# The first three pairs of weight loads move to ScalarE's DMA queue, and the weight conversions start one attention unit sooner

## The chip, the core and the metric

The kernel runs on one core of a Trainium2 chip. Its time is the device time of one execution in microseconds; the kernel before has a median of 679.96 us over three runs (679.66 to 681.74). A profile is one further execution, recorded instruction by instruction; its durations are compared with its own span, not with the median.

The engines are called as in the profile: PE is TensorE (matmuls; PEld are its weight loads), DVE is VectorE, ACT is ScalarE, POOL is GpSimd and SP is SyncE, which here does nothing but start DMA transfers. SPq and ACTq are the queues of SP and ACT seen as starters of transfers.

## The reference

What is computed is a decaying linear attention, whose result goes straight into a feed-forward layer with a softplus:

```python
state = zeros((B, H, D, D))                       # B, H, S, D = 4, 8, 768, 64
for t in range(S):
    state = gamma[:, None, None] * state + outer(k[:, :, t], v[:, :, t])
    y[:, :, t] = D ** -0.5 * (q[:, :, t] @ state)
x = y.transpose(0, 2, 1, 3).reshape(B * S, H * D) # 3072 tokens x 512
h = x @ w_in                                      # 512 x 2048
out = softplus(h) @ w_out                         # 2048 x 512
```

q, k and v are float32. The weights w_in and w_out are float64, and each load brings their 64-bit words as they are.

## The kernel before

**Attention units.** The sequence of a batch is cut into six chunks of 128 tokens, and each chunk into two halves of four heads: 48 units, worked one after the other. The first twelve units load q, k and v by tokens (`load_unit`, L148 to L164; the DMA itself is L153, 128 KB each for kn, qn and vn). On the way to its output a unit needs, in this order: POOL multiplies q and v by decay factors (L172, L177); PE transposes k and q (`operands`, L186, tile tp); ACT and DVE copy them out of PSUM (kz L188 and L189, qs L190); PE forms the scores (`scores`, L217, tile sc); ACT copies them (L218, tile a); POOL masks them (L225); PE multiplies by v (`outputs`, L280 and L283, tile yp); ACT and DVE split the result into two float32r parts, xh (L284) and xl (L285). `new_state` (L245, tile stp) and `stack_state` (L261, stw) carry the state from chunk to chunk.

**The feed-forward part.** The 2048 hidden columns are cut into 16 slices f of 128. For a block of 256 or 384 tokens, `hidden` (L330 to L332, tile hp) multiplies xh and xl by the slice of w_in, ACT and DVE form the softplus (L337 to L346, tiles sp, gh, gl), and `second` (L361 to L363, tile acc) multiplies by the slice of w_out. The first block of 256 tokens can start when the units of its first two chunks have their xh and xl, that is after units 0 to 3; the first hp matmuls need units 0 and 2 alone. The block takes slices 0 to 9 first, then the second block all sixteen.

**Weights.** `load_weights(f)` starts two transfers of 512 KB: 128 columns of w_in (L70, tile win) and 128 rows of w_out (L71, tile wout). `convert_weights(f)` makes from the 64-bit words two float32r tiles, winhl and wouthl, each a high and a low part: ACT scales the high words (L86, and L92 for wout), DVE shifts and joins (L94 to L96), ACT rounds to the high part (L98), and POOL subtracts to get the low part (L99). A slice costs five instructions on ACT's list, five on DVE's and two on POOL's. From slice FETCH = 3 on, a load is held until the ACT cast L98 of three slices earlier is done (the "pace" dependency).

**Order.** The program is written as ticks, four to a unit (`tick`, L314 to L318). Before the first feed-forward step a loop runs the ticks for the first units and starts weight loads and conversions between them; in it, slice 0 is loaded when the tick counter stands at -5, slices 1 and 2 at 3 and 7, and from 11 on each fourth tick converts a slice and loads another: slice 0 at 11, slice 1 at 15, slice 2 at 19. After that `convert_to` keeps the conversions ahead of the steps. A scheduler, which sorts by its own estimate of when things are ready, lays the written order out as one list for each engine, and each engine works strictly down its list.

**Waits of transfers.** Every transfer signals one of eight completion counters, DMAHW0 to DMAHW7, given out in turn. A transfer that takes a counter over waits at its place in the list until the transfer that had it before has landed. What stands behind it in the same list waits with it.

Of the kernel before, what the change touches and what calls it, by code (L numbers as in the profile page):

```python
# [17 lines left out]
P = 128  # L18
# [10 lines left out]
FETCH = 3  # L29
# [4 lines left out]
def decay_attention_then_softplus_ffn(ctx: ExitStack, tc: tile.TileContext, q, k, v, w_in, w_out, qtab, vtab, gtab, out):  # L34
    nc = tc.nc
# [3 lines left out]
    ND = DM // P  # L39
# [24 lines left out]
    raw, win, wout, converts = {}, {}, {}, {}  # L64

    def load_weights(f):
        fs = slice(f * P, (f + 1) * P)
        raw[f] = [const.tile([P, ND * P], I64, name=nm, tag=f"{nm}{f}") for nm in ("win", "wout")]
        loads_of_f = (
            nc.sync.dma_start(raw[f][0].rearrange("p (c w) -> p c w", c=ND), w_in[:, fs].rearrange("(c p) w -> p c w", p=P)),  # L70
            nc.sync.dma_start(raw[f][1], w_out[fs, :]),  # L71
        )

        if f >= FETCH:
            for load, after in zip(loads_of_f, converts[f - FETCH]):
                tc.add_manual_dep(load.ins, after.name, mybir.DependencyInfo(mybir.DependencyClass.Sync, mybir.DependencyReason.SCHED_ONLY), reason="pace")
# [237 lines left out]
    def tick(n):  # L314
        for at, part in PARTS.items():
            u, r = divmod(n - at, PERIOD)
            if r == 0 and 0 <= u < len(units):
                part(u)  # L318
# [69 lines left out]
    def ticks_for(i):  # L388

        return min(PERIOD * 2 * int(FIRST[i + 1] // C) + max(PARTS) - PERIOD + 1 + AHEAD, last_tick + 1)  # L390

    done, loaded, converted = FIRST_TICK, 0, 0

    def convert_to(n):
        nonlocal loaded, converted
        while converted < min(NF, n):
            convert_weights(converted)
            converted += 1
            if loaded < NF:
                load_weights(loaded)  # L400
                loaded += 1
# [6 lines left out]
    nc.scalar.dma_start(vtabs[:, 0], vtab)  # L408
    nc.scalar.dma_start(gtab_sb[lo, 0], gtab)
    nc.scalar.dma_start(gtab_sb[up, 0], gtab)  # L410
    make_identity(nc, ident)
    for par, own, oth in sides:
        nc.gpsimd.memset(kz[oth, par], 0.0)
# [24 lines left out]
    while done < ticks_for(0):  # L438
        tick(done)
        done += 1  # L440
        if done % 4 == 3 and done > 0 or done < 0 and loaded == 0:
            if loaded >= FETCH:
                convert_weights(converted)
                converted += 1
            load_weights(loaded)
            loaded += 1

# [69 lines left out]
```

## Time and profile before

| | us |
|---|---|
| median of three runs | 679.96 |
| the profiled execution | 688.11 |
| its span, first to last instruction | 686.0 |
| PE busy in the span | 661.4 |
| DVE / ACT / POOL busy | 433.2 / 357.2 / 315.0 |

The profiled execution is 8.15 us longer than the median, and 2.1 us of it lie outside the span. All times below are counted from the span's start. In a row of the timeline the columns are: start, duration, engine, line, operation, output and inputs, and in brackets the idle time of the engine just before it with what ended that. A duration of several merged instructions is that of the group. In a row of windows the columns are: the window, its length, the busy time of each engine with the number of instructions, the granted PE clock, the busy share of the 16 DMA engines and the rate in GB/s.

### The profile page before, as it was taken

The numbers are of one execution on the slowest core, as the hardware profiler recorded it, in microseconds if no ns is written. First come the engines' busy times: TensorE is split into PE (matmuls) and PEld (weight loads), VectorE is DVE, ScalarE is ACT, GpSimd is POOL, SyncE is SP. The second block draws the span as 40 slices with busy tenths as digits, with TensorE's granted clock in tenths as the row PEclk, the third lists the DMA queues.
The fourth block names the chain that finished last, engine by engine and source line by source line (L and its number), as shares of the span: only waits on it lengthen the run. The fifth ranks groups of instructions, "written<-read, shape, count | busy, mean of one in ns | idle before, by whom it ended". The sixth has DMA issues, their size and how long they took to land.

```text
span 686.0 us, 12848 instructions
## 1 busy us (share of the span) xinstructions
PE 661.4 (96%) x4136; PEld 601.1 (88%) x4136; DVE 433.2 (63%) x843; ACT 357.2 (52%) x808; POOL 315.0 (46%) x354
## 2 busy tenths in 40 slices
PE   6899999998999999999999899999999899999997
PEld 5788898988999899989999899999999799999996
DVE  5777788677556676775676766786656755432321
ACT  5787766545454555654555555564555545422221
POOL 5787667534343544454355344545343443332221
PEclk9999999999999999999999999999999999999999
DMA  8897561222221241222122122222222111000100
GB/s 241 221 292 215 164 177 36 50 68 67 46 38 36 37 102 30 40 40 71 37 39 55 35 78 42 36 50 41 73 38 39 34 31 47 1 1 0 47 1 32
DMA packets 153827, 46.76 MB, mean 68 GB/s; under 512 B 140448, under 2 KB 148640, under 8 KB 153760
## 3 DMA queue, kind: packets, MB, share of 16 engines
q1 hardware_dynamic: 153312, 45.93, 28.1%
q8 instruction: 33, 0.54, 0.3%
q14 instruction: 34, 0.28, 0.1%
q10 hardware_dynamic: 448, 0.01, 0.0%
HBM read 39.60 MB, written 6.29 MB: 67 GB/s over the span
## 4 chain that ended last, share of the span: by engine, by line
PE 70%; SPq 8%; DMA 8%; DVE 5%; issue 4%; ACT 3%; POOL 2%; POOLq 0%; DVEq 0%; ACTq 0%
PE hp L330 10%; PE hp L332 10%; PE hp L331 10%; PE acc L361 10%; PE acc L363 10%; PE acc L362 10%; SPq L136 7%; DMA win<-in_moe_w_in_dram 2%; DMA vn<-in_v_dram 2%; PE sc L223 2%; PE stp L245 2%; DMA qb<-in_q_dram 1%; DVE kq L200 1%; PE yp L296 1%; PE yp L297 1%
## 5 line engine op out<-in xcount | busy, mean ns | idle before, releaser
L346 POOL TENSOR_TENSOR gl<-sp,gh 128x384 fp32r<-128x384 f32 (+1 forms) x120 | 130.8, 1090 | 227.8 <-ACT gh L344 198.9
L330 PE MATMUL hp<-xh,winhl 128*128 128x384 f32 (+1 forms) x576 | 186.0, 323 | 2.1 <-DVE sp L342 0.9
L332 PE MATMUL hp<-xh,winhl 128*128 128x384 f32 (+1 forms) x576 | 185.3, 322 | 0.9 <-POOL winhl L99 0.9
L331 PE MATMUL hp<-xl,winhl 128*128 128x384 f32 (+1 forms) x576 | 184.7, 321 | 0.0
L361 PE MATMUL acc<-wouthl,gh 128*128 128x512 f32 x384 | 153.1, 400 | 0.2 <-ACT gh L344 0.2
L362 PE MATMUL acc<-wouthl,gh 128*128 128x512 f32 x384 | 151.8, 396 | 0.0
L363 PE MATMUL acc<-wouthl,gl 128*128 128x512 f32 x384 | 150.7, 396 | 0.1
L338 ACT ACTIVATE sp<-sp 128x384 f32<-128x384 f32 (+1 forms) x120 | 65.3, 545 | 138.0 <-DVE sp L337 137.8
L330 PEld LDWEIGHTS hp<-xh,winhl 128*128 128x128 f32 x576 | 109.4, 190 | 6.5 <-ACT winhl L98 1.0
L331 PEld LDWEIGHTS hp<-xl,winhl 128*128 128x128 f32 x576 | 109.5, 190 | 3.8
L332 PEld LDWEIGHTS hp<-xh,winhl 128*128 128x128 f32 x576 | 109.4, 190 | 1.6 <-POOL winhl L99 1.3
L337 DVE TENSOR_SCALAR sp<-hp 128x384 uint32<-128x384 uint32 (+1 forms) x120 | 68.6, 574 | 63.2 <-PE hp L332 62.0
L344 ACT CAST gh<-sp 128x384 fp32r<-128x384 f32 (+1 forms) x120 | 64.0, 534 | 74.0 <-DVE sp L342 50.1
L342 DVE SCALAR_TENSOR_TENSOR sp<-hp,sp 128x384 f32<-128x384 f32 (+1 forms) x120 | 69.5, 579 | 35.8 <-ACT sp L338 34.9
L363 PEld LDWEIGHTS acc<-wouthl,gl 128*128 128x128 f32 x384 | 71.9, 188 | 14.8 <-POOL gl L346 0.5
L361 PEld LDWEIGHTS acc<-wouthl,gh 128*128 128x128 f32 x384 | 72.4, 189 | 11.1 <-ACT gh L344 0.3
L362 PEld LDWEIGHTS acc<-wouthl,gh 128*128 128x128 f32 x384 | 72.5, 189 | 10.8
L225 POOL TENSOR_SCALAR_AFFINE_SELECT a<-a 128x512 f32<-128x512 f32 x48 | 35.1, 730 | 43.2 <-DVE a L224 39.3
L224 DVE TENSOR_REDUCE a<-sc 128x256 f32<-128x512 f32 x72 | 48.8, 679 | 7.1 <-PE sc L223 4.1
L230 POOL TENSOR_TENSOR al<-a,ah 128x512 fp32r<-128x512 f32 x36 | 47.8, 1327 | 9.3 <-ACT ah L229 9.1
L200 DVE TENSOR_TENSOR kq<-kb,kq 64x256 fp32r<-64x256 f32 x72 | 45.3, 629 | 3.2 <-ACT kq L199 1.0
L195 DVE STREAM_TRANSPOSE kb<-kb 128x256 f32<-128x256 f32 x36 | 16.0, 445 | 49.3 <-DMA kb<-in_k_dram 37.9
(81 smaller groups left out, 993.1 us busy)
## 6 DMA issues: line engine op xcount, KB each, us to landing
win<-in_moe_w_in_dram SPq DMA_DIRECT2D x16, 512.0 KB, 5.0
wout<-in_moe_w_out_dram SPq DMA_DIRECT2D x16, 512.0 KB, 4.5
vn<-in_v_dram SPq DMA_DIRECT2D x48, 128.0 KB, 2.8
out_dram<-o SPq DMA_DIRECT2D x24, 256.0 KB, 2.2
kb<-in_k_dram SPq DMA_DIRECT2D x288, 16.0 KB, 1.7
qb<-in_q_dram SPq DMA_DIRECT2D x288, 16.0 KB, 1.7
vn<-in_k_dram SPq DMA_DIRECT2D x30, 128.0 KB, 2.3
kn<-in_k_dram SPq DMA_DIRECT2D x12, 128.0 KB, 3.9
```

What stands on the lines that cost most here:

```text
L200: nc.vector.tensor_tensor(kq[oth, 0, par], kt[own], kq[own, 0, par].bitcast(F32), op=ALU.subtract)
L330: nc.tensor.matmul(hp[:, k], lhsT=wt[:, 0, d, :], rhs=xh[:, d, :], start=d == 0, stop=False)
L331: nc.tensor.matmul(hp[:, k], lhsT=wt[:, 0, d, :], rhs=xl[:, d, :], start=False, stop=False)
L332: nc.tensor.matmul(hp[:, k], lhsT=wt[:, 1, d, :], rhs=xh[:, d, :], start=False, stop=d == ND - 1)
L337: nc.vector.tensor_scalar(sp.bitcast(U32), hps[s].bitcast(U32), 0x80000000, None, op0=ALU.bitwise_or)
L338: nc.scalar.activation(sp, sp, AF.Softplus)
L342: nc.vector.scalar_tensor_tensor(g, hps.pop(s), 0.0, g, op0=ALU.max, op1=ALU.add)
L344: nc.scalar.copy(gh, g)
L346: nc.gpsimd.tensor_tensor(gl, sps.pop(s), gh.bitcast(F32), op=ALU.subtract)
L361: nc.tensor.matmul(acc[i][t], lhsT=gh[:, k, ts], rhs=wt[:, 0], start=begins and k == 0, stop=False)
L362: nc.tensor.matmul(acc[i][t], lhsT=gh[:, k, ts], rhs=wt[:, 1], start=False, stop=False)
L363: nc.tensor.matmul(acc[i][t], lhsT=gl[:, k, ts], rhs=wt[:, 0], start=False, stop=ends and f == fs[-1])
```

## The change

The transfers of slices 0, 1 and 2 are started by ACT, right behind the four small table loads with which ACT's list begins, instead of by SP between the loads of the first units. The loop of ticks then converts and loads from counter 7 on, so slices 0 to 3 are converted at 7, 11, 15 and 19 (before: slices 0 to 2 at 11, 15 and 19).

```diff
@@ load_weights(f)
+        queue = nc.scalar if f < FETCH else nc.sync
         loads_of_f = (
-            nc.sync.dma_start(raw[f][0]..., w_in[:, fs]...),
-            nc.sync.dma_start(raw[f][1], w_out[fs, :]),
+            queue.dma_start(raw[f][0]..., w_in[:, fs]...),
+            queue.dma_start(raw[f][1], w_out[fs, :]),
         )
@@ after the four table loads on nc.scalar
+    for _ in range(FETCH):
+        load_weights(loaded)
+        loaded += 1
@@ while done < ticks_for(0):
         tick(done)
         done += 1
-        if done % 4 == 3 and done > 0 or done < 0 and loaded == 0:
-            if loaded >= FETCH:
-                convert_weights(converted)
-                converted += 1
+        if done % 4 == 3 and done > 4 * FETCH - 8:
+            convert_weights(converted)
+            converted += 1
             load_weights(loaded)
             loaded += 1
```

In the changed kernel all lines behind the first edit have numbers that are higher by 1 to 4. The lists below give, for each place, the row of the list, the line, the operation with its tiles (a number behind a name tells copies of a tile apart), and in brackets the counters and engines waited for.

**ACT at the start of the program.** Before, the first copy of unit 0 stands behind the table loads:

```order
L409 DMA gtab_sb_77<-in_gtab_dram 64x8
L410 DMA gtab_sb_77<-in_gtab_dram 64x8
L188 COPY kz_86<-tp_140 64x256 [waits PE_49]
L190 COPY qs_87<-tp_140 128x256 [waits DVE_49]
L261 COPY stw0_88<-stp_93 64x2x64 [waits DVE_49]
L218 COPY a_155<-sc_156 128x512 [waits PE_49]
L86 ACTIVATE win_134<-win_134 128x512 [waits DMAHW2_49]
```

And now:

```order
L411 DMA gtab_sb_77<-in_gtab_dram 64x8
L71 DMA win_108<-in_moe_w_in_dram 128x4x128 [waits DMAHW1_49]
L72 DMA wout_109<-in_moe_w_out_dram 128x512 [waits DMAHW3_49]
L71 DMA win_112<-in_moe_w_in_dram 128x4x128 [waits DMAHW5_49]
L72 DMA wout_113<-in_moe_w_out_dram 128x512 [waits DMAHW7_49]
L71 DMA win_116<-in_moe_w_in_dram 128x4x128 [waits DMAHW1_49]
L72 DMA wout_117<-in_moe_w_out_dram 128x512 [waits DMAHW3_49]
L189 COPY kz_86<-tp_148 64x256 [waits PE_49]
L262 COPY stw0_88<-stp_93 64x2x64 [waits DVE_49]
L87 ACTIVATE win_108<-win_108 128x512
L87 ACTIVATE wout_109<-wout_109 128x512
L191 COPY qs_87<-tp_148 128x256 [waits DVE_49]
```

Six transfers now stand ahead of the first copy. Counters 1, 3, 5 and 7 are those of ACT's four table loads; the third win takes over counter 1 from the first win, and the third wout counter 3 from the first wout. The activations of win_108 and wout_109 have no wait of their own any more, because ACT has waited for both landings by then.

**SP behind the loads of units 0 and 1.** Before, the rows from the last load of unit 1 on are:

```order
L153 DMA vn1_91<-in_v_dram 128x4x64 [waits DMAHW1_49]
L70 DMA win_134<-in_moe_w_in_dram 128x4x128 [waits DMAHW2_49]
L71 DMA wout_135<-in_moe_w_out_dram 128x512 [waits DMAHW3_49]
L153 DMA kn_148<-in_k_dram 128x4x64 [waits DMAHW4_49,PE_49]
L153 DMA qn_150<-in_q_dram 128x4x64 [waits DMAHW5_49,Pool_49]
L153 DMA vn2_92<-in_v_dram 128x4x64 [waits DMAHW6_49]
L70 DMA win_163<-in_moe_w_in_dram 128x4x128 [waits DMAHW7_49]
```

Now the loads of unit 2 follow those of unit 1 directly, then seven small loads of a table (qblocks), and then come these rows, the last two of the seven first:

```order
L434 DMA qblocks_80<-in_qtab_dram 32x4x1 [waits DMAHW0_49]
L434 DMA qblocks_80<-in_qtab_dram 32x4x1 [waits DMAHW1_49]
L71 DMA win_223<-in_moe_w_in_dram 128x4x128 [waits DMAHW2_49,Activation_49]
L434 DMA qblocks_80<-in_qtab_dram 32x4x1 [waits DMAHW3_49]
L154 DMA kn_190<-in_k_dram 128x4x64 [waits DMAHW4_49,PE_49]
L154 DMA qn_192<-in_q_dram 128x4x64 [waits DMAHW5_49,PE_49,Pool_49]
```

win_223 is slice 3, and kn_190 and qn_192 belong to unit 3. The row of qblocks ahead of kn_190 takes counter 3, which the third wout on ACT had before it.

**ACT around the first softplus.** Slice 4's cast is `winhl_517` in both. Before, it stands behind the first two softplus activations and the first gh:

```order
L338 ACTIVATE sp_404<-sp_404 128x512 [waits DVE_49]
L86 ACTIVATE win_373<-win_373 128x512 [waits DMAHW4_49]
L188 COPY kz_86<-tp_467 64x256 [waits PE_49]
L344 CAST gh_408<-sp_404 128x512 [waits DVE_49]
L338 ACTIVATE sp_459<-sp_459 128x512 [waits DVE_49]
L284 CAST xh_82<-yp_475 128x2x128 [waits PE_49]
L86 ACTIVATE wout_374<-wout_374 128x512 [waits DMAHW1_49]
L98 CAST winhl_517<-w_513 128x512 [waits DVE_49]
```

And now:

```order
L87 ACTIVATE win_337<-win_337 128x512 [waits DMAHW6_49]
L262 COPY stw1_89<-stp_93 64x2x64 [waits DVE_49]
L285 CAST xh_82<-yp_351 128x2x128 [waits PE_49]
L219 COPY a_369<-sc_370 128x512 [waits PE_49,Pool_49]
L99 CAST wouthl_392<-w_388 128x512 [waits DVE_49,Activation_49]
L87 ACTIVATE wout_338<-wout_338 128x512 [waits DMAHW1_49]
L99 CAST winhl_517<-w_513 128x512 [waits DVE_49]
L93 ACTIVATE wp_521<-wout_280 128x512
L339 ACTIVATE sp_426<-sp_426 128x512 [waits DVE_49]
```

Slice 4's cast has moved ahead of the first softplus, and xh of unit 3 (made from `yp_351`) has slice 5's first activation (`win_337`) ahead of it. On PE the two lists differ up to about row 490 of 3942, matmul by matmul; behind that they are the same.

More of the change, by code (lines that the diff above doesn't have):

```diff
@@ L68, in load_weights @@
         raw[f] = [const.tile([P, ND * P], I64, name=nm, tag=f"{nm}{f}") for nm in ("win", "wout")]
+        queue = nc.scalar if f < FETCH else nc.sync
         loads_of_f = (
-            nc.sync.dma_start(raw[f][0].rearrange("p (c w) -> p c w", c=ND), w_in[:, fs].rearrange("(c p) w -> p c w", p=P)),
-            nc.sync.dma_start(raw[f][1], w_out[fs, :]),
+            queue.dma_start(raw[f][0].rearrange("p (c w) -> p c w", c=ND), w_in[:, fs].rearrange("(c p) w -> p c w", p=P)),
+            queue.dma_start(raw[f][1], w_out[fs, :]),
         )
```

## The prediction

> **What bounds the kernel now.** I read the busy times of the page first, then the engines by stages.
>
> ```profile
> PE 661.4 (96%) x4136; PEld 601.1 (88%) x4136; DVE 433.2 (63%) x843; ACT 357.2 (52%) x808; POOL 315.0 (46%) x354
> 0.00:35.00 35.00, 25.14 (x162) 22.63 (x163) 21.82 (x51) 22.84 (x47) 22.84 (x42) 0.95 0.87 233
> 35.00:60.00 25.00, 24.79 (x176) 22.47 (x175) 19.27 (x34) 20.59 (x43) 21.35 (x27) 1.00 0.93 262
> 60.00:82.00 22.00, 19.68 (x154) 18.56 (x153) 16.53 (x30) 15.36 (x32) 12.52 (x13) 1.00 0.69 200
> 82.00:686.00 604.00, 591.74 (x3652) 537.44 (x3651) 375.61 (x730) 298.41 (x688) 258.31 (x273) 0.99 0.21 46
> ```
>
> PE is the bound: 661.4 of 686.0 us. An edit that leaves PE's work alone moves the end by what it adds to PE's idle time or takes from it. The second column shows where that idle time lies: 9.86 us (35 - 25.14) up to 35 us, 0.21 to 60, 2.32 to 82, 12.26 in the 604 us behind. PE's list is the same in both kernels behind its row 490, so the matter is decided in the first 80 us, where 12.4 us can be won at most.
>
> The first stage is a ramp of four attention units. Its steps, unit by unit, are read in the timeline:
>
> ```profile
> 5.66 0.37 ACT L188 COPY kz<-tp 64x256 f32<-64x256 f32 x1 [3.57 <-PE tp L186]
> 10.52 0.34 ACT L188 COPY kz<-tp 64x256 f32<-64x256 f32 x1
> 12.88 0.62 ACT L98 CAST winhl<-w 128x512 fp32r<-128x512 f32 x1 [0.30 <-DVE w L96]
> 20.73 0.66 PE L186 MATMUL tp<-ident,kn 128*128 128x128 f32 x2 [1.85 <-DVE wp L95]
> 22.11 0.36 ACT L188 COPY kz<-tp 64x256 f32<-64x256 f32 x1
> 24.15 0.37 ACT L284 CAST xh<-yp 128x256 fp32r<-128x256 f32 x1 [1.68 <-PE yp L283]
> 24.41 0.38 ACT L190 COPY qs<-tp 128x256 f32<-128x256 f32 x1
> 24.84 1.16 PE L217 MATMUL sc<-qs,kz 128*128 128x128 f32 x8
> 30.92 0.48 PE L330 MATMUL hp<-xh,winhl 128*128 128x256 f32 x2
> ```
>
> ACT's copy kz marks a unit: 5.66 for the first, 10.52 for the second, 22.11 for the fourth. (The cast at 12.88 is slice 0's.) From the fourth unit's scores at 24.84 on PE has feed-forward work beside the units and hardly stops. PE's three stops of 0.6 us or more between 30 and 125 us are these:
>
> ```profile
> 64.81 0.39 PE L330 MATMUL hp<-xh,winhl 128*128 128x256 f32 x1 [0.81 <-ACT winhl L98]
> 65.95 0.49 PE L280 MATMUL yp<-qs,stw 128*128 128x128 f32 x2 [0.64 <-ACT a L218]
> 79.83 0.35 PE L330 MATMUL hp<-xh,winhl 128*128 128x256 f32 x1 [0.87 <-DVE sp L342]
> ```
>
> The first is a wait for a weight slice. The second is its consequence: ACT's copy a stands behind the same conversion.
>
> **Term 1: ACT is held at the start.** In the new list ACT's first copy stands behind six transfers, the sixth of which takes over its counter from the first wout. So ACT does nothing for unit 0 until that wout has landed. That such a wait holds a list is seen on SP, whose fifth load went out at 3.45, when kn of 0.81 had landed:
>
> ```profile
> 0.81 2.62 DMA kn<-in_k_dram
> 3.45 0.37 SPq L153 DMA_DIRECT2D qn<-in_q_dram  x1
> L408 ACTq DMA_DIRECT2D vtabs<-in_vtab_dram x1: 517/517/517, 1.3 to 1.3; - x1
> DMA to landing us min/median/max: 2.7/2.7/2.7
> L71 SPq DMA_DIRECT2D wout<-in_moe_w_out_dram x1: 503/503/503, 5.0 to 5.0; - x1
> DMA to landing us min/median/max: 6.3/6.3/6.3
> L71 SPq DMA_DIRECT2D wout<-in_moe_w_out_dram x14: 340/401/1860, 5.0 to 83.7; - x14
> DMA to landing us min/median/max: 3.2/4.6/8.0
> ```
>
> The first wout of the new list takes its counter from the table vtabs, which lands at 1.3 + 2.7 = 4.0. The three landing lines are those of vtabs, of the first wout now (issued at 5.0), and of all wout loads up to 84 us; each stands under its transfer. With the 6.3 us of the first wout, which shares the transfers of units 0 and 1 with the new one, it lands at 10.3; the issue of the last load, 0.5 us (503 ns in the row of the first wout), frees ACT at 10.8. The kz of unit 0 comes 10.8 - 5.66 = **5.1 us** later. Bounds: 4.0 + 3.2 + 0.5 gives 2.0 us, 4.0 + 8.0 + 0.5 gives 6.8 us. It can't be below: kz stands in the same list. Nothing covers it, since scores, mask and output of unit 0 all follow from that copy. The six issues cost SP's list less, but nobody waits there for it.
>
> **Term 2: more conversions between the units.** From the first kz to the fourth unit's qs ACT's list had 26 instructions and now has 30, as conversions stand one unit earlier. At the 0.5 us by which conversions follow each other (64.16 to 64.66 below) four cost 2.0 us where ACT never waits and nothing where it would wait anyway. In the list's first unit it has to wait for DVE's part of slice 0, now between kz and a; later ACT has slack. I take **+0.8**, bounds 0 and 2.0.
>
> **Term 3: the wait of the fourth unit goes.** The row at 20.73 names DVE's wp, but the matmul list asks for counter 4 there, which is unit 3's kn:
>
> ```profile
> 12.71 1.08 SPq L153 DMA_DIRECT2D kn<-in_k_dram  x1
> DMA to landing us min/median/max: 7.9/7.9/7.9
> L153 SPq DMA_DIRECT2D kn<-in_k_dram x5: 368/438/1084, 0.8 to 20.7; - x5
> DMA to landing us min/median/max: 2.6/3.2/7.9
> 2.00:22.00 20.00, 12.92 (x70) 10.94 (x71) 11.29 (x31) 11.76 (x26) 11.69 (x19) 0.96 0.98 267
> ```
>
> 12.71 + 7.9 = 20.6: the load took 7.9 us, 3.2 is the median of the first five kn, and the 16 DMA engines were 0.98 busy from 2 to 22 us. In the changed kernel this load stands behind a table row that takes its counter from the third wout, issued at 10.3; with 6.3 us that lands at 16.6, kn goes out at 17 and lands at 20.2 with 3.2 us or 24.9 with 7.9. The units are by then 5 to 6 us late, so PE would ask for it at about 18.88 + 5.1 = 24.0 (18.88 is where the group before the row of 20.73 ended, 20.73 - 1.85). The wait of **1.85** goes with the median and shrinks to 0.9 with the longest. I take the median, as slices 0 to 2 have landed by then.
>
> The Trainium skill speaks against this term: DMA: Bandwidth & Descriptors, section "Issuing engines are not separate DMA queues", says that transfers begun by different engines run on the same 16 DMA engines and interleave, so that a second starter only saves issue time. The 0.98 agrees; by it alone kn stays at 7.9 us, and the sum below would be 0.95 higher.
>
> **Term 4: qs before xh.** Now qs of unit 3 (24.41) stands behind xh of unit 2, before which ACT idled 1.68 us. The new list has qs first. kz to sc was 2.73 us (22.11 to 24.84); with kz, DVE's copy and qs alone it was 1.28 in unit 0 (5.66 to 6.94), 1.45 less, but a conversion's two instructions now stand between. **-0.9**, bounds 0 and -1.45.
>
> Sum at the fourth unit's scores: 5.1 + 0.8 - 1.85 - 0.9 = 3.15. Between there and the row at 30.92 PE is nearly always busy, and one group of the next unit, which stood behind that row, has moved ahead of it:
>
> ```profile
> 42.33 0.45 PE stp L245 x4
> ```
>
> This is such a group in the chain of waits (start, length, what), 0.45 us. So PE is 3.15 - 0.45 = **+2.7 us** late when it gets dense.
>
> **Term 5: the stop at 64.81 closes.** ACT's conversions run in a loop through the DMA:
>
> ```profile
> 57.29 0.62 ACT L98 CAST winhl<-w 128x512 fp32r<-128x512 f32 x1
> 58.20 0.46 SPq L70 DMA_DIRECT2D win<-in_moe_w_in_dram  x1
> 63.59 0.66 ACT L86 ACTIVATE win<-win 128x512 f32<-128x512 f32 x1 [1.87 <-DMA win<-in_moe_w_in_dram]
> 64.16 0.60 ACT L98 CAST winhl<-w 128x512 fp32r<-128x512 f32 x1
> 64.66 0.63 ACT L92 ACTIVATE wp<-wout 128x512 uint32<-128x512 uint32 x1
> 71.03 0.62 ACT L98 CAST winhl<-w 128x512 fp32r<-128x512 f32 x1
> ```
>
> A cast releases the load of three slices later, and its first activation stands in ACT's list ahead of the next cast: 57.29, 64.16, 71.03, one slice in 6.9 us, most of it the transfer. This loop runs by its own time. In the changed list slice 4's cast stands ahead of the first softplus, so the loop is no later than now while PE comes 2.7 us later: the 0.81 and the 0.64 go, **-1.45**. If the loop moves with PE, they stay. The 0.87 at 79.83 comes from the softplus and I leave it.
>
> Sum: +2.7 - 1.45 = **+1.25 us**. The profiled execution would take 688.11 + 1.25 = 689.4; carried over to the median, which lies 8.15 us lower, 679.96 + 1.25 = **681.2 us**. A measurement of this kernel can tell about 0.3% from no change, 2.0 us, so the forecast is "no change", on the slow side.
>
> **The rivals.** *Slower, by the held ACT.* The loop of conversions moves with PE (ACT's copy a, which waits for PE, stands in the loop too), and the two stops stay: 679.96 + 2.7 = 682.7; with the wout at 8.0 us 684.4. It decides from the point at which the first wout lands later than 10.3 or slice 8's cast comes later than now relative to PE. For it: a transfer of 6 to 8 us is usual there (the DMA engines are 0.98 busy). Against: the new place of slice 4's cast.
>
> A second price on this side is PE's clock:
>
> ```profile
> 6.94 2.07 PE L217 MATMUL sc<-qs,kz 128*128 128x128 f32 x8 [0.21 <-ACT qs L190]
> 12.34 1.16 PE L217 MATMUL sc<-qs,kz 128*128 128x128 f32 x8 [0.79 <-ACT qs L190]
> 20.00:24.00 4.00, 3.27 (x16) 3.21 (x16) 3.64 (x7) 1.96 (x4) 3.68 (x5) 0.57 1.02 254
> ```
>
> The same scores took 2.07 us at first and 1.16 later, and behind the idle 1.85 us the granted clock fell to 0.57 over 20 to 24 us. A longer idle start can add one more such stretch, 2.07 - 1.16 = 0.9 us: 682.1. The Trainium skill, TensorE: Matmul & The Clock Gate, section "What's actually happening", says the clock is halved until PE has been busy for about 3.4 us; the two rows agree with a factor near two.
>
> *Faster.* The first wout lands as soon as its shortest allows or little later (ACT free at 8.5, term 1 of 2.8), and with the weights ahead all three stops go: 2.7 - 2.3 - 1.45 - 0.87 = -1.9, 678.0. For it: ACT's queue is asked first and its transfers need not stand behind those of unit 1. Against: DMA engines without a gap.
>
> *The change does not bring the weights sooner.* Slice 0's cast started at 12.88 before; held to 10.8, ACT cannot cast it before activation and DVE's three steps, some 3 us, so about 13.8. I expect this in all cases: for the first three slices "sooner" is in the program's order, not in time.
>
> **How the numbers follow.** Forecast (679.5 to 682.0) 0.45; held ACT or clock, over 682.0, 0.36; faster, under 677.9, 0.19, of which the bulk lies close to the forecast's lower side. The range takes the faster case down to 678.0 and the slower one up to its 684.4, and leaves out the ends of each: 678.0 to 684.4. Chances: faster by over 0.3% 0.19, within 0.45, slower 0.36.
>
> **What would show it.** Right: ACT's first kz at about 10.8 (7.7 to 12.5), later kz at about +5 to +6, no wait for unit 3's kn, unit 3's scores near 28.0, PE's first dense hp near 33.6, no stop of PE at the ninth slice. Wrong: kz before 7.7, a stop at the ninth slice as before, PE's idle time behind 82 us changed by more than 1 us, or kn of unit 3 landing behind its need.

## The result and the profile after

| | before | changed |
|---|---|---|
| median of four runs, us | 680.85 (679.66 to 682.00) | 689.20 (688.01 to 689.39) |
| ratio, with 95% interval | | 1.0119 (1.0095 to 1.0144) |
| the profiled execution, us | 688.11 | 689.1 |
| its span, us, and mean granted PE clock | 686.0, 0.992 | 687.1, 1.000 |

The changed kernel is 8.35 us slower by the medians. The forecast was 681.2 us and "no change"; the time lies outside the range of 678.0 to 684.4.

The two profiled executions differ by 1.1 us in span only; that of before ran at a granted clock of 0.992. So the comparison that follows uses marks: the same row of the program in both traces, at an early place. (The granted clock can differ ahead of a mark too: from 20 to 24 us it was 0.57 in the kernel before and 1.00 in the changed one.) A late and a good one is the first matmul of scores against all keys (row 619 of PE's list in every kernel here). In the timeline, first before, then changed:

```profile
122.48 0.48 PE L223 MATMUL sc<-kq 128*128 128x256 f32 x2
```

```profile
129.20 0.48 PE L224 MATMUL sc<-kq 128*128 128x256 f32 x2
```

PE arrives 6.7 us later. This is nearly the whole loss, and it was made earlier than that. The page's busy line of the changed kernel and the windows that were read before (window, its length, busy time of PE, PEld, DVE, ACT and POOL, granted clock, share of the DMA engines, GB/s):

```profile
PE 658.7 (96%) x4136; PEld 598.4 (87%) x4136; DVE 431.6 (63%) x843; ACT 357.9 (52%) x808; POOL 314.7 (46%) x354
```

```profile
0.00:35.00 35.00, 19.62 (x106) 16.61 (x107) 18.47 (x45) 18.99 (x39) 18.72 (x37) 1.00 0.80 214
35.00:60.00 25.00, 23.68 (x178) 22.32 (x178) 18.04 (x33) 19.36 (x40) 18.61 (x25) 1.00 0.83 239
60.00:82.00 22.00, 21.53 (x163) 20.27 (x162) 15.85 (x29) 16.88 (x36) 17.56 (x19) 1.00 0.75 216
82.00:687.00 605.00, 593.82 (x3695) 539.22 (x3693) 379.21 (x739) 302.69 (x696) 259.80 (x276) 1.00 0.22 47
```

PE is idle for 15.38 us up to 35 us (9.86 before), and the DMA engines are busy for 0.80 of that stretch instead of 0.87. From 82 us on its idle time is 11.2 us (12.3 before): little has happened there. The ramp, unit by unit, is in ACT's and POOL's timeline:

```profile
9.64 0.61 POOL L173 TENSOR_TENSOR qn<-qn,qtabs 128x256 f32<-128x256 f32 x1 [4.04 <-DMA qn<-in_q_dram]
10.73 0.37 ACT L189 COPY kz<-tp 64x256 f32<-64x256 f32 x1 [8.64 <-DMA wout<-in_moe_w_out_dram]
11.48 1.19 PE L246 MATMUL stp<-vn,kn 128*128 128x128 f32 x4 [4.61 <-POOL vn L178]
14.35 0.61 POOL L173 TENSOR_TENSOR qn<-qn,qtabs 128x256 f32<-128x256 f32 x1 [3.00 <-DMA qn<-in_q_dram]
16.25 0.35 ACT L189 COPY kz<-tp 64x256 f32<-64x256 f32 x1
23.75 0.36 ACT L189 COPY kz<-tp 64x256 f32<-64x256 f32 x1
29.17 0.35 ACT L189 COPY kz<-tp 64x256 f32<-64x256 f32 x1
31.23 1.06 PE L218 MATMUL sc<-qs,kz 128*128 128x128 f32 x8
```

ACT's kz of units 0 to 3 comes 5.1, 5.7, 8.0 and 7.1 us later than before (5.66, 10.52, 15.72, 22.11). The hold of ACT is there, as forecast. But POOL stands idle for 4.04 us and then for 3.00 us, waiting for q of units 1 and 2 to land, and PE for 4.61 us, waiting for unit 1's v (which POOL had to scale first). Before, POOL's two waits were 0.53 and 2.26 us:

```profile
5.98 0.61 POOL L172 TENSOR_TENSOR qn<-qn,qtabs 128x256 f32<-128x256 f32 x1 [0.53 <-DMA qn<-in_q_dram]
12.61 0.61 POOL L172 TENSOR_TENSOR qn<-qn,qtabs 128x256 f32<-128x256 f32 x1 [2.26 <-DMA qn<-in_q_dram]
```

The loads themselves show it. These are SP's transfers of q and v of unit 1, issued from 3.4 to 3.9, and of q, k and v of unit 2, issued behind them, with the time from issue to landing. Before:

```profile
L153 SPq DMA_DIRECT2D vn<-in_v_dram x1: 505/505/505, 3.9 to 3.9; - x1
DMA to landing us min/median/max: 2.5/2.8/3.1
L153 SPq DMA_DIRECT2D kn<-in_k_dram x1: 368/368/368, 6.8 to 6.8; - x1
DMA to landing us min/median/max: 5.1/5.2/5.2
```

And in the changed kernel:

```profile
L154 SPq DMA_DIRECT2D vn<-in_v_dram x1: 411/411/411, 3.9 to 3.9; - x1
DMA to landing us min/median/max: 6.2/6.5/6.8
L154 SPq DMA_DIRECT2D kn<-in_k_dram x1: 368/368/368, 6.9 to 6.9; - x1
DMA to landing us min/median/max: 8.3/8.7/10.5
```

A load of 128 KB that took 2.5 to 3.1 us takes 6.2 to 6.8 us, one that took 5.2 takes 8.3 to 10.5. The chain of the work that ended last (start, length, what) has the load of unit 2's q as its longest piece of the ramp:

```profile
5.52 8.67 DMA qn<-in_q_dram
14.96 1.24 POOL winhl L100
16.85 2.07 PE yp L284 x8
```

It is the longest chain by little. ACT had copied unit 0's scores at 15.79, and POOL, busy with the late q and a conversion, masked them from 16.15 on: here unit 2's late q costs 0.36 us at most. PE's wait for unit 1's v ended at 11.48, and unit 0's scores had to wait until 13.09 for ACT's qs as well. From there to unit 2's kz the delay grows by another 1.9 us, and these rows of PE and ACT show where:

```profile
13.09 2.07 PE L218 MATMUL sc<-qs,kz 128*128 128x128 f32 x8 [0.42 <-ACT qs L191]
16.85 2.07 PE L284 MATMUL yp<-a,vn 128*128 128x128 f32 x8 [0.83 <-POOL a L226]
19.68 1.87 PE L218 MATMUL sc<-qs,kz 128*128 128x128 f32 x8
21.39 0.38 PE L187 MATMUL tp<-ident,kn 128*128 128x128 f32 x2
21.64 0.59 ACT L219 COPY a<-sc 128x512 f32<-128x512 f32 x1 [2.31 <-PE sc L218]
22.12 0.67 ACT L87 ACTIVATE wout<-wout 128x512 f32<-128x512 f32 x1
22.68 0.61 ACT L99 CAST winhl<-w 128x512 fp32r<-128x512 f32 x1
23.19 0.63 ACT L93 ACTIVATE wp<-wout 128x512 uint32<-128x512 uint32 x1
```

From 16.85 to 21.39 PE works without a wait, on matmuls that take up to twice their usual time. Then unit 2's k and q are transposed (tp), but ACT's list has three instructions of conversions ahead of kz, which comes 2.36 us after its tp started. Before, it came 0.76 us after it:

```profile
14.96 0.44 PE L186 MATMUL tp<-ident,kn 128*128 128x128 f32 x2 [1.46 <-ACT a L218]
15.72 0.37 ACT L188 COPY kz<-tp 64x256 f32<-64x256 f32 x1 [0.22 <-PE tp L186]
```

### The profile page after: what moved, and what is told of

Its sections match the earlier page's. It is cut to its first block, busy times and chain, and to the rows that moved or that the text cites. A ratio compares the mean times of both kernels' runs of the same rounds, so it can differ in the third digit from the quotient of the medians.

```text
span 687.1 us, 12838 instructions
## 1 busy us (share of the span) xinstructions
PE 658.7 (96%) x4136; PEld 598.4 (87%) x4136; DVE 431.6 (63%) x843; ACT 357.9 (52%) x808; POOL 314.7 (46%) x354
## 4 chain that ended last, share of the span: by engine, by line
PE 63%; DMA 10%; SPq 9%; DVE 8%; issue 4%; ACT 3%; POOL 2%; DVEq 0%; ACTq 0%; POOLq 0%
PE hp L333 9%; PE hp L331 9%; PE hp L332 9%; PE acc L362 9%; PE acc L364 9%; PE acc L363 9%; SPq L137 8%; DVE kq L201 2%; DMA win<-in_moe_w_in_dram 2%; DMA kb<-in_k_dram 2%; DMA vn<-in_v_dram 2%; DMA qn<-in_q_dram 2%; PE stp L246 2%; PE sc L224 2%; SPq L154 1%
```

## The experiments

Four theories were set against each other. **T**, traffic: the weights requested in the first 10 us take the transfers' time from q, k and v of units 1 and 2. **H**: ACT is held until the first wout lands. **S**: SP's list is held by completion counters, so that unit 3's loads go out late. **C**: conversions one unit sooner crowd ACT and POOL. Each is read at four places of the ramp: kz of units 0 and 2, the scores of unit 3 (which end the ramp) and the first scores against all keys. The column conv. counts the instructions of conversions that stand in ACT's list ahead of unit 2's kz. The ratio is that of the medians to the kernel before, run on the same chip, with its 95% interval. The last column says whether PE's list from row 490 on is in the order of the kernel before (third_behind: from row 574 on).

| kernel | kz 0 | kz 2 | scores 3 | all keys | conv. | ratio | order |
|---|---|---|---|---|---|---|---|
| before (its two profiles) | 5.66, 5.76 | 15.72, 15.35 | 24.84, 23.97 | 122.48, 121.01 | 5 | 1 | same |
| changed (its two profiles) | 10.73, 10.63 | 23.75, 23.70 | 31.23, 30.38 | 129.20, 128.86 | 11 | 1.0119, 1.0122 | same |
| late_convert | 10.55 | 23.55 | 31.41 | 129.91 | 11 | 1.0076 (1.0049 to 1.0103) | same |
| sync_queue | 5.76 | 21.04 | 29.17 | 129.03 | 12 | 1.0068 (1.0042 to 1.0093) | same |
| extra_loads | 5.62 | 19.66 | 28.29 | 129.25 | 4 | 1.0110 (1.0073 to 1.0148) | same |
| qblocks_late | 11.84 | 24.33 | 30.80 | 130.15 | 11 | 1.0101 (1.0063 to 1.0140) | same |
| one_pair_tables | 5.84 | 17.43 | 24.62 | 121.79 | 7 | 1.0022 (0.9998 to 1.0047) | same |
| third_behind | 5.69 | 15.64 | 21.24 | 123.51 | 5 | 0.9995 (0.9966 to 1.0025) | same |
| queue_only | 6.02 | 20.05 | 30.45 | 129.67 | 8 | 1.0097 (1.0059 to 1.0135) | other |
| two_pairs | 6.51 | 22.59 | 28.86 | 127.46 | 11 | 1.0075 (1.0039 to 1.0111) | other |
| convert_only | 5.99 | 17.54 | 23.07 | 123.38 | 7 | 1.0117 (1.0058 to 1.0175) | other |
| before_qlate | 5.63 | 15.21 | 23.36 | 120.17 | 5 | 1.0058 (1.0019 to 1.0096) | other |
| one_pair | 5.87 | 17.02 | 24.21 | 122.75 | 7 | 1.0096 (1.0064 to 1.0127) | other |

Two things keep these runs from moving one thing alone. With each edit the scheduler laid out the ramp anew, up to row 490 of PE's list and on the other engines beside it, so that in most of them the conversions moved too. And the granted clock differs: from 20 to 30 us it was 0.50 in sync_queue and in queue_only, 0.84 in extra_loads and 1.00 in the changed kernel.

**before_again.** The kernel before without an edit, because its profiled execution lay 8.15 us above its median.

> The kernel before, unchanged, for a second profile. The first profiled execution took 688.1 us against a median of 680.9, with a granted clock of 0.992 on average and of 0.57 from 20 to 24 us. Theory A (that execution lost its time to the granted clock): a profile at clock 1.00 has a span of 678 to 680 us, PE busy about 658.7 us as in the changed kernel's profile, and PE idle about the same 12 us up to 82 us. Theory B (recording the profile costs the kernel before 6 to 8 us that it doesn't cost the changed one): the span is 686 us again.

Measured: 685.34 us median (683.01 to 687.15, 8 runs), 1.0008 (0.9975 to 1.0041) of the 24 runs of the same kernel beside it, which went from 680.1 to 690.24. So this kernel scatters by 10 us. Much of it goes with the granted clock: over the 84 runs of it in these experiments the 22 with a mean clock of 0.999 or 1.000 took 682.6 us on average, the 5 with 0.990 to 0.993 took 687.8. Theory B, that recording costs time, does not hold: the second profiled execution took 685.2 us, as much as the median of its runs. Theory A was not put to its test, as that execution ran at 0.994 and not at 1.00. The marks up to 122 us agree within 1.5 us.

**queue_only.** The edit of the queue in load_weights alone, with the calls left at their places:

```diff
+        queue = nc.scalar if f < FETCH else nc.sync
-            nc.sync.dma_start(raw[f][0]..., w_in[:, fs]...),
-            nc.sync.dma_start(raw[f][1], w_out[fs, :]),
+            queue.dma_start(raw[f][0]..., w_in[:, fs]...),
+            queue.dma_start(raw[f][1], w_out[fs, :]),
```

> The kernel before with one edit: the loads of slices 0 to 2 are started by ACT, at the places in the program where they stood; conversions as before. Theory H (ACT held at its first copy until the first wout lands is the cost): unit 0's kz comes at about 5.7 as before, its copy a is held to about 10.5 instead of 9.05, so about +1.5 us, 681 to 683. Theory T (the ACT queue's transfers take half of the DMA engines' turns, so that units 1 and 2 get their q, k and v 4 to 7 us later): as the changed kernel, 687 to 690, with qn of unit 1 landing at 9 to 10. Theory S (table loads on SP wait behind ACT's transfers through the counters, and unit 3's loads behind them): unit 3's loads here stand behind four table rows only, issue at 16 to 18 us, 684 to 687. Theory C (conversions one unit sooner crowd ACT and POOL): no change, 679 to 682.

Measured: 690.74 us, and at unit 3's scores and at all keys the marks of the changed kernel within 0.8 us, without the other edits. The scheduler puts the six loads near the head of ACT's list even so, since nothing there holds them; kz of unit 0 comes at 6.02 and that of unit 2 at 20.05. The run does not decide between the theories: ACT is held in part (its copy a of unit 0 came at 11.55, 9.05 before), and the clock of 0.50 falls into the ramp.

**late_convert.** The changed kernel with the conversions at the counters of before:

```diff
-        if done % 4 == 3 and done > 4 * FETCH - 8:
+        if done % 4 == 3 and done > 4 * FETCH - 4:
```

> The changed kernel with the conversions where they stood before (counter at 11, 15, 19); the six loads stay up front on ACT. Theories H, T and S: 687 to 691 as the changed kernel, since the start of the lists is the same. Theory C: 680 to 683.

Measured: 689.54 us and the four marks of the changed kernel within 0.8 us. But this run does not test C. The scheduler sorts by when it takes things to be ready, and laid out PE's, ACT's and DVE's lists row for row as in the changed kernel; only three rows of POOL's list and two of SP's differ. So the conversions ran where they ran there. In the same way, with only the conversions written one unit sooner, the kernel before keeps its order on all five engines. It is the early loads that bring the conversions forward, and C stays open here.

**sync_queue.** The changed kernel with all six loads on SP's queue, behind those of units 0 and 1; nothing holds ACT:

```diff
-        queue = nc.scalar if f < FETCH else nc.sync
+        queue = nc.sync
```

> The changed kernel with the six loads up front on SP instead of ACT, behind the loads of units 0 and 1; conversions one unit sooner. Theory H: no hold, kz of unit 0 at 5.7, 679 to 682. Theory T: units 0 and 1 undisturbed, unit 2's k, q and v stand behind 3 MB and land at 15 to 17 instead of about 12, so unit 2 is up to 2 us late, 681 to 683. Theory S: table rows stand behind unit 3's loads here, 679 to 682. Theory C: 686 to 690.

Measured: 689.18 us. Unit 0 and unit 1 are where they were before (5.76 and 10.22), yet unit 2's kz comes at 21.04 and all keys at 129.03. So a loss of this size arises without the hold of ACT. H, S and T had expected at most 683 us, T with unit 2 up to 2 us late where it is 5.3 to 5.7; the time is within C's 686 to 690. PE's timeline in this run shows what is late instead:

```profile
16.91 0.41 PE L187 MATMUL tp<-ident,kn 128*128 128x128 f32 x2 [3.77 <-DVE wp L96]
20.31 0.69 PE L187 MATMUL tp<-ident,qn 128*128 128x128 f32 x2 [1.96 <-POOL qn L173]
```

Unit 2's transposes wait 3.77 and 1.96 us. (The first row names DVE's wp, but the k that it needs, issued at 8.09, landed at about 16.9, if it took the longest of the times that follow.) Its loads, issued from 8.1 to 10.2 behind 3 MB of weights in the same queue, took 7.8 to 8.8 us to land (5.1 to 5.2 before, issued from 6.8 to 7.7). But q, issued at 8.57, had landed by 17.4, and POOL took it up at 19.64 only, behind a conversion of slice 1:

```profile
18.41 1.27 POOL L100 TENSOR_TENSOR winhl<-w,winhl 128x512 fp32r<-128x512 f32 x1 [0.87 <-ACT winhl L99]
19.64 0.62 POOL L173 TENSOR_TENSOR qn<-qn,qtabs 128x256 f32<-128x256 f32 x1
```

So the late loads and the early conversions both have a part in it. From unit 2's scores on the clock of 0.50 comes on top (these scores took 2.08 us, 1.16 in the changed kernel), so that the agreement with the changed kernel at all keys is in part chance.

**extra_loads.** The kernel before with three further transfers from ACT, 1.5 MB in all, which nobody reads:

```diff
     nc.scalar.dma_start(gtab_sb[up, 0], gtab)
+    for f in (10, 11, 12):
+        extra = const.tile([P, ND * P], I64, name="extra", tag=f"wout{f}")
+        nc.scalar.dma_start(extra, w_out[f * P:(f + 1) * P, :])
```

> The kernel before, with three further transfers of 512 KB each (rows of w_out into buffers that nobody reads before their own later load) started by ScalarE behind its three tables. ScalarE is held only by a table's landing (about 5 us), no conversion moves. T (early weight traffic makes the loads of units 1 and 2 land late): the kz copy of unit 2, at 15.3 to 15.7 before and 23.75 in the changed kernel, comes at 19 or later, and the first scores against all keys, 121.0 to 122.5 before and 129.2 changed, at 124 to 129. H (held ScalarE) and C (conversions sooner): kz of unit 2 within 1 us of before, first scores against all keys at 121 to 123.5.

Measured: 690.84 us; units 1 and 2 late (kz at 14.02 and 19.66), all keys at 129.25. ACT's first copy came at 5.62, and no conversion came forward: four stand ahead of unit 2's kz, five before. In POOL's and ACT's timeline:

```profile
5.62 0.37 ACT L188 COPY kz<-tp 64x256 f32<-64x256 f32 x1 [3.53 <-PE tp L186]
8.95 0.61 POOL L172 TENSOR_TENSOR qn<-qn,qtabs 128x256 f32<-128x256 f32 x1 [3.32 <-DMA qn<-in_q_dram]
19.66 0.37 ACT L188 COPY kz<-tp 64x256 f32<-64x256 f32 x1 [0.91 <-PE tp L186]
```

The wait of 3.32 us for unit 1's q is close to that of the changed kernel (4.04). This run adds bytes, where the change only moves them, and slice 0 lands later in it; that the loss is as large shows that traffic can suffice, not that it is all of the change's loss.

**convert_only.** The kernel before with the pairs of slices 1 and 2 one unit sooner on SP, slice 1's ahead of unit 2's loads, and conversions one unit sooner:

```diff
-        if done % 4 == 3 and done > 0 or done < 0 and loaded == 0:
+        if done in (-5, -1) or done % 4 == 3 and done > 0:
```

> The kernel before with conversions one unit sooner (slice 0 between units 0 and 1) and the loads left on SyncE's queue, two pairs ahead of unit 1's and unit 2's places and the third at its new place. C (conversions sooner crowd ScalarE and GpSimd): kz of unit 2 at 20 or later, first scores against all keys at 127 to 130. T: what comes late follows the traffic, which is one pair sooner only: kz of unit 2 at 16 to 19, first scores against all keys at 121.5 to 126. H: as before, 121 to 123.

Measured: kz of unit 2 at 17.54 and all keys at 123.38, as T has it for one pair; C had expected 20 or later and 127 to 130. In the list two conversions more stand ahead of unit 2's kz, where the changed kernel has six more. The time is 691.13 us, which the ramp does not explain; see one_pair.

**two_pairs.** The changed kernel with only slices 0 and 1 on ACT's queue, slice 2 on SP's:

```diff
-        queue = nc.scalar if f < FETCH else nc.sync
+        queue = nc.scalar if f < 2 else nc.sync
...
-    for _ in range(FETCH):
+    for _ in range(2):
...
+        if done == 3:
+            load_weights(loaded)
+            loaded += 1
```

> The changed kernel with two pairs on ScalarE's queue at the start and the third on SyncE's between the units; no counter holds ScalarE beyond a table's landing, near 5.5. T: 1 MB less stands ahead of unit 2's loads; kz of unit 2 at 17 to 21 and the first scores against all keys at 123 to 127. H: kz of units 0 and 2 as before (5.7, 15.5), first scores at 121 to 123. C: as the changed kernel, 128 to 130, since the conversions stand as there.

Measured: kz of unit 0 at 6.51, so no hold there; of unit 1 at 16.12 and of unit 2 at 22.59, all keys at 127.46. T had too small numbers for it: with the same two pairs on SP's queue (convert_only) unit 2's kz came at 17.54. What the second queue adds is that the weights run beside unit 1's loads instead of behind them: POOL waited 3.71 us for unit 1's q. ACT had copied qs of unit 0 by 10.1, and PE came to unit 0's scores at 13.12 all the same (13.09 in the changed kernel), because unit 1's stp stands ahead of them and waited for v:

```profile
12.11 1.22 PE L246 MATMUL stp<-vn,kn 128*128 128x128 f32 x4 [5.24 <-POOL vn L178]
13.12 1.92 PE L218 MATMUL sc<-qs,kz 128*128 128x128 f32 x8
```

Behind that the conversions (eleven ahead of unit 2's kz, as in the changed kernel) are not told apart from the traffic.

**after_again.** The changed kernel again, on the chip of the last three.

> The changed kernel again, on the chip of the three others, to have the size of the difference beside runs of the same hour: kz of units 0, 1, 2 near 10.7, 16.3, 23.8, first scores against all keys near 129, time over that of the kernel before 1.007 to 1.013 by every theory.

Measured: 690.90 us against 683.30, ratio 1.0122 (1.0073 to 1.0171), marks within 1.2 us of the first profile up to 130 us.

**qblocks_late.** The changed kernel with the sixteen small table loads of SP moved behind the fifth conversion:

```diff
-                nc.sync.dma_start(
+                qb = nc.sync.dma_start(
...
+                tc.add_manual_dep(qb.ins, converts[4][0].name, ...)
```

> The changed kernel with the sixteen small table loads of SyncE's list moved behind the fifth conversion, so that the loads of unit 3 no longer stand behind the counters that these ask for. S (the held list makes unit 3 late): kz of unit 2 stays at 23 to 24.5, unit 3's loads go out at 11 to 13, its kz comes before 28, and the first scores against all keys at 124 to 127. T (traffic): the same kz of unit 2, kz of unit 3 within 1 us of 29, first scores against all keys at 128 to 130.

Measured: unit 3's loads go out at 16.7 and 17.2 instead of 21.3 and 21.9, and nothing is won by it at the mark: all keys at 130.15, ratio 1.0101. S falls as the cause of the loss. SP's hold is real and leaves the DMA engines idle (0.27 busy from 16 to 22 us in the changed kernel, 0.84 in this one). Unit 3's kz does gain by its end: it comes 3.64 us after unit 2's, where it came 5.42 after it, and at 27.97 just within what S had expected. But unit 0's kz was 1.1 us later here, and what was gained is gone at all keys.

**before_qlate.** The same edit on the kernel before.

> The kernel before with the sixteen small table loads behind the fifth conversion, nothing else. If small transfers cost the ramp (the 16 engines handle many packets for them): kz of unit 3, 21.4 to 22.1 before, 1 to 2 us sooner, first scores against all keys at 119 to 121. If bytes alone decide: kz of unit 3 within 0.5 us, first scores against all keys at 121 to 122.5.

Measured: all keys at 120.17, 0.8 to 2.3 us sooner, but 688.41 us, ratio 1.0058 (1.0019 to 1.0096): a quicker ramp and a slower kernel.

**third_behind.** The opposite of the change: the kernel before, tables late, and slice 2's pair behind unit 3's loads in SP's list.

```diff
+        if f == 2:
+            for load in loads_of_f:
+                for after in went[3]:        # k and q loads of unit 3
+                    tc.add_manual_dep(load.ins, after, ...)
```

> The opposite of the change: the kernel before with the small table loads late as in before_qlate, and the pair of slice 2 behind the k, q and v of unit 3 on SyncE's queue. T: the ramp gains what the pair no longer takes ahead of unit 3: its kz (21.4 to 22.1) at 18 to 20, first dense feed-forward work (23.7 to 24.6) at 21 to 23, first scores against all keys at 118 to 121, time 1 to 3 us under that of the kernel before. H and C: nothing of this kernel bears on them, marks within 1 us of before_qlate.

Measured: 684.92 us, ratio 0.9995 (0.9966 to 1.0025). Unit 3's scores come at 21.24 (23.97 and 24.84 before), and its kz at 19.96, as T had it, but the first feed-forward matmul at 24.20 only, and all keys at 123.51, where T had 118 to 121 and a shorter time. The gain at unit 3 is lost behind it; where stays open.

**one_pair.** The changed kernel with slice 0's pair alone on ACT's queue:

```diff
-        queue = nc.scalar if f < FETCH else nc.sync
+        queue = nc.scalar if f < 1 else nc.sync
...
-    for _ in range(FETCH):
+    for _ in range(1):
...
+        if done in (3, 7):
+            load_weights(loaded)
+            loaded += 1
```

> The changed kernel with the pair of slice 0 alone on ScalarE's queue at the start and those of slices 1 and 2 on SyncE's, behind the loads of unit 2; conversions as in the changed kernel. T, and its second half (a pair on the second queue runs beside unit 1's loads, where on SyncE's queue it stood behind them): unit 2's loads no longer wait for weights, kz of unit 1 at 10.5 to 13, of unit 2 at 16 to 19, first scores against all keys at 121 to 124.5. If the second queue itself costs, whatever its amount: kz of unit 1 at 15 or later as with two pairs, first scores against all keys at 126 to 129. C: 127 to 130, since the conversions stand as in the changed kernel.

Measured: all keys at 122.75, the ramp of before again. Yet 691.85 us, ratio 1.0096. Behind the mark it took 567.4 us (690.2 - 122.75) at a mean clock of 0.994, the changed kernel 557.9 at 1.000; by the averages above the clock accounts for some 4 us of the 9.5. The lists say why this could be: in one_pair, before_qlate, convert_only, two_pairs and queue_only the scheduler also chose another order of PE's list up to row 1806. These are the idle times before the scores against all keys from 122 us on (total, times), in one_pair:

```profile
  DVE a L225: 16.9, 15
```

in before_qlate:

```profile
  DVE a L224: 16.4, 12
```

and in the changed kernel:

```profile
  DVE a L225: 7.4, 6
```

(PE and PEld are counted together; PE's own are 7.1, 7.1 and 3.1 us, and 4.1 in the kernel before.) In the kernels of the other order these scores wait about twice as long for DVE's reduction a; whether that is the whole of the rest was not shown. This is no part of the change, whose own list is in the old order there.

**one_pair_tables.** To tell that apart: one_pair with the tables late, which brings the order back. Against qblocks_late only the place and queue of the pairs of slices 1 and 2 differ:

```diff
-        queue = nc.scalar if f < FETCH else nc.sync
+        queue = nc.scalar if f < 1 else nc.sync
...
-    for _ in range(FETCH):
+    for _ in range(1):
...
+        if done in (3, 7):
+            load_weights(loaded)
+            loaded += 1
```

> The kernel of one_pair with the small table loads behind the fifth conversion, by which the order of PE's list behind its row 490 is again that of the kernel before and of the changed kernel (with one_pair alone it differs up to row 1806). Against qblocks_late the only difference is that the pairs of slices 1 and 2 go by SyncE behind unit 2's loads. T: first scores against all keys at 120.5 to 123.5, time over that of the kernel before 0.997 to 1.003, against 1.010 in qblocks_late. If one_pair's later loss (567.4 us behind its first scores against all keys, where the changed kernel took 557.9) comes from the pair on ScalarE's queue and not from the order of PE's list: scores at 122 to 123 again and 1.006 to 1.012.

Measured: 684.75 us, ratio 1.0022 (0.9998 to 1.0047), against 1.0101 (1.0063 to 1.0140) of qblocks_late. Unit 3's scores and all keys:

```profile
24.62 1.06 PE L218 MATMUL sc<-qs,kz 128*128 128x128 f32 x8
121.79 0.48 PE L224 MATMUL sc<-kq 128*128 128x256 f32 x2
```

With the order as before, taking two of the three pairs out of the first 10 us takes the loss away, at the mark (8.4 us against qblocks_late) and in the time. That takes away ACT's hold too (unit 0's kz at 5.84 against 11.84), and four of the eleven conversions ahead of unit 2's kz, so this run does not say which of the three it was. It took 557.3 us behind the mark (679.1 - 121.79, at a clock of 1.000), so the pair alone does not cause one_pair's later loss. It doesn't beat the kernel before, from which it can't be told apart.

## Why the prediction was wrong

**What bounds the kernel: right.** PE's idle time behind 82 us fell by 1.1 us, just more than the 1 us that was named as a sign of being wrong, but it fell, and the loss was made in the ramp.

**Term 1, ACT held: right.** ACT's first kz came at 10.73; 10.8 was predicted. Its scores came at 13.09, 6.15 us later than before (6.94), as two activations had also moved ahead of qs.

**Term 2: this step failed.** It let units 1 and 2 follow the hold with nothing but 0.8 us of more conversions (at most 2.0). The measured delay grows from 5.07 us at unit 0's kz to 8.03 at unit 2's, by 2.96 us. In the changed kernel's trace the parts are these: 1.08 to unit 0's scores, for the two activations ahead of qs; 0.30 to unit 0's yp, at POOL's mask; 0.89 to unit 1's scores, as yp took 2.07 us and not 1.16; 0.91 less to unit 2's tp, where a wait of 1.46 us is gone and slower scores stand in its place; 1.60 to unit 2's kz, for the three instructions of conversions ahead of it. So some 2.7 us are the term's own mechanism, mis-sized. It counted four conversions more on the whole way to unit 3's qs and let three fifths of them vanish in ACT's waits; but at unit 2's kz six more have passed (eleven against five), and there the unit did wait for them.

**What it left out** is what the transfers do to units 1 and 2: 3 MB of weights were requested in the first 10.4 us, and q, k and v of these units shared the engines with them. The prediction had this at hand twice. It let the *weights* land late because they share the transfers with units 0 and 1, and did not ask what the sharing does to units 0 and 1. And it set the Trainium skill's rule (DMA: Bandwidth & Descriptors, section "Issuing engines are not separate DMA queues": transfers begun by different engines run on the same DMA engines) against unit 3's load alone, though the same holds for the loads of units 1 and 2. The trace agrees with that rule: unit 1's loads went from 2.5 to 3.1 us to 6.2 to 6.8 when ACT started weights beside them.

**Hold and traffic cover each other.** In the changed kernel unit 0's scores stand behind both unit 1's stp, which waited for the late v and started at 11.48, and ACT's qs, which was copied at 13.04. In two_pairs qs was done by 10.1 and the late v alone brought these scores to 13.12, as late as the 13.09 of the changed kernel. So without the hold, which the prediction took for the price of the change, little would have been won there. sync_queue and extra_loads are as late at all keys without that hold, with the reservations above. A hold without the traffic was not run, and no run has the traffic of the change without its early conversions: how the loss divides between these two stays open.

**Term 3, unit 3's wait: half right.** The wait for kn is gone, and in the way that was named: kn went out at 21.27 (17 predicted), and the loads of unit 3 took 3.5 to 3.6 us (3.2 predicted), so that it was there before its transpose at 26.58. But only 0.97 us were gained (8.03 us late at unit 2's kz, 7.06 at unit 3's) where 1.85 was predicted. Right ahead of unit 3's kz ACT now waits for the wout of slice 3:

```profile
28.60 0.67 ACT L87 ACTIVATE wout<-wout 128x512 f32<-128x512 f32 x1 [1.18 <-DMA wout<-in_moe_w_out_dram]
```


**Term 4: right.** From kz to the scores of unit 3 it now takes 2.06 us (29.17 to 31.23), 0.67 less; 0.9 was predicted.

**The sum at unit 3's scores**: +3.15 predicted, 31.23 - 24.84 = +6.39 measured. The missing 3.2 us are those of term 2 (2.2 more than predicted), of term 3 (0.9) and of term 4 (0.2).

**Term 5: the stops close, others open.** The stops at 64.81 and 65.95 are gone, as predicted, and that at 79.83 too. In their place PE stops in the changed kernel at

```profile
63.79 0.74 PE L364 MATMUL acc<-wouthl,gl 128*128 128x512 f32 x2 [0.47 <-POOL gl L347]
84.18 0.44 PE L187 MATMUL tp<-ident,kn 128*128 128x128 f32 x2 [1.00 <-ACT a L219]
```

PE's stops of this kind from 42 to 125 us sum to 2.32 us before (0.81, 0.64 and 0.87) and 1.47 now, so 0.85 us were won, where 1.45 was predicted. Ahead of that PE lost more than before, in two waits for ACT's copy stw of 0.59 and 1.31 us; before, its one wait behind unit 3's scores was 0.32. The second of them is

```profile
39.12 0.71 PE L246 MATMUL stp<-vn,kn 128*128 128x128 f32 x4 [1.31 <-ACT stw L262]
```

So from unit 3's scores (6.39 us late) to those against all keys (6.72 late) nothing is made up in the end.

**The rivals.** "Held ACT" had the right sign, and its price of 2.7 to 4.4 us was too small for the reason of term 2. PE's slow start did cost: yp of unit 0 took 2.07 us and unit 1's scores 1.87, where both took 1.16 before, about 1.6 us of longer matmuls, which PE worked off without a wait between them on the way to unit 2's kz; 0.9 was the price named. "The weights do not come sooner" was right: slice 0's cast came at 13.93 (12.88 before; 13.8 predicted) and slice 1's at 22.68 (18.84 before).

**The time carried over.** Adding the sum to the median was sound. By the marks (+6.4 at unit 3's scores, +6.7 at all keys) the median would be 686.7; it was 689.2 against 680.85. The rest is within the scatter of such medians: the changed kernel's two runs at a clock of 1.000 took 689.1 and 689.3, and the 22 runs of before at 0.999 and 1.000 took 682.6 on average, 6.6 us less.

## What to carry to other kernels

Where the DMA engines are nearly always busy, a load that is moved ahead is paid for by the loads that it passes or runs beside: price the transfers of every unit in the stretch, not only the one whose wait was to go. Request early what is needed first; here the weights of slices 1 and 2 were needed after units 1 and 2, and their lead bought nothing. And compare the kernels at marks inside the trace, and the lists of every engine, both where the edit is and far behind it: a scheduler can leave an experiment without effect (late_convert), move other instructions along with the one that was meant, or change an order behind the edit that has nothing to do with its purpose.

## What the runs showed of the hardware that was not expected

- Unit 1's loads of 128 KB took 2.5 to 3.5 us with up to six transfers of 512 KB behind them in their own queue (before, convert_only, sync_queue), and 5.9 to 7.1 us when a second queue had such transfers under way (two_pairs; 6.2 to 6.8 in the changed kernel).
- The DMA engines went from 0.96 to 0.27 busy from 16 to 22 us in the changed kernel, because SP's list took 9.23 us over seven 0.5 KB table loads, which stand in it with waits for completion counters (the last of them waits for one that the third win of the other queue had before it):

```profile
10.69 9.23 SPq L434 DMA_DIRECT2D qblocks<-in_qtab_dram  x7
```

- Runs of the kernel before differ with the granted clock by 5 us of 680 on average (682.6 us at 0.999 to 1.000, 687.8 at 0.990 to 0.993), not much less than the change. One profiled execution may lie 8 us above the median, as that of before did.
- PE's matmuls of the first units take up to twice as long (2.07 against 1.16 us for the same eight) at a granted clock of 1.00, and as long (2.08) at one of 0.50 in sync_queue, so that this clock does not show every slow stretch. Before, the first such group of 1.16 us started at 10.40; in the changed kernel, where PE waited 4.61 us ahead of 11.48, a group that started at 19.68 still took 1.87.
